# Attention and an ELU layer on one core: the order of the loads, the bank pair of unit 3, and the engines' written orders of two blocks

## The chip, the core and the metric

The kernel runs on one core of one Trainium2 chip. The metric is the device time of one execution in microseconds (us). The profile is of one execution; its engines are TensorE (PE, with its weight loads as PEld), VectorE (DVE), ScalarE (ACT), GpSimd (POOL) and SyncE (SP). All times below, unless said otherwise, count from the start of the profiled span.

## The reference: what is computed

A linear attention over 8 batches x 8 heads x 576 rows x 64 columns, and behind it a layer of 512 to 2048 to 512 with an ELU between, for all 4608 rows:

```python
q_s = softmax of q over the 64 columns
k_s = softmax of k over the 576 rows
kv  = einsum('bhsd,bhde', transposed k_s, v)      # 64 x 64 for each head
x   = (q_s @ kv) with the heads side by side       # 4608 x 512
h   = x @ w_in                                     # 512 -> 2048
g   = h where h > 0, else exp(min(h, 0)) - 1
out = g @ w_out                                    # 2048 -> 512
```

Inputs and output are float32. (The two softmax lines are in words; the maxima that the reference takes off first are not needed with inputs of this size.)

## The kernel before: how the work is laid out

**Units.** The attention is done in 16 units. A unit is four of the eight heads of one batch (`n // 2` is the batch, `n % 2` the half): q, k and v tiles of 128 x 1152, 576 KB each. For a unit, ScalarE takes the exponentials of q and k; VectorE sums q (`L421`) and takes the RECIPROCAL (`L423`); Pool or VectorE makes the quotient in 16 bits (`L433`, tile QS); Pool or ScalarE turns v to bf16 (`stage1`, `L277`, tile VB). Then the quotient is transposed: for units 0 to 3 on TensorE into PSUM (`tp`, `L457`) and copied out to qsT (`L277`), for the later ones by a DMA from SP (`turn`, `L470`, tile QT) and a widening copy (`widen`, `L277`). TensorE multiplies k by v (`kv_mm`, `L507`), VectorE divides by the sums of k and writes the 64 x 64 results into a block mask (`m`, `L516` and `L520`, tile MBLK), TensorE multiplies mask and transposes (`ao_mm`, `L538`; for units 0 and 1 `ao_parts`, `L550`), in two parts called outputs below, and ScalarE or VectorE copies these into XT (`xt`, `L277`), the input of the layer.

**Blocks.** The layer is done in nine blocks of 512 rows. A block has eight groups: a group is 8 matmuls on W1 into a pair of PSUM banks (`hg_mm`, `L620`), then the ELU (`hg`): the exponential on ScalarE (`L646`), and either a Relu on ScalarE and one operation on VectorE (`L648`, `L652`) or two on VectorE (`L657`, `L659`). The results are in GR. Blocks 0 and 1 multiply GR by W2 in the plain way (`out_mm`, `L673`): block 0 in four tiles of rows (ts) by four quarters of W2, 4 matmuls each; block 1 in pieces of two. From block 2 on, a scheme with sums and differences does it (`pair`, `L806`, `L757`, `L815`).

**Banks.** PSUM has 8 banks, b0 to b7, in four pairs. b6 and b7 (AB = 3 in `program`) are the side banks, which the attention takes from unit 2 on; b4 and b5 (C = 2) serve the groups and the rows' outputs and are lent to the attention here and there. Before, unit 3's transposes and its first output use b4 and b5; its product of k and v and its second output use b6 and b7.

**Order.** The program makes a list of operations, `S.ops`, each with what it reads and writes. The order on each engine is written out by hand in `ORDER`, as numbers of that list; `order()` times it with costs only to interleave the engines and to place spare matmuls at the start (`fill`, `spare_until`), and `emit()` puts in the waits. So an engine runs its line in the written order, and an instruction that waits holds up all that stand behind it on its engine. DMAs issued by Pool (`load`, `load_w1`, `load_w2`) stand in Pool's line among its copies and products and run one behind the other; later loads, the turns and the stores are issued by SP. `AFTER` adds four waits on Pool, which are the same operations before and after the change.

The numbers below are those of before. What matters of them:

- 14 to 17: W1 for groups 0 to 2, one for each 128 of its 512 rows; 18, 19, 20, 21: W1 for group 3, 4, 5, and 6 with 7. 69, 70, 74, 75: W2's four quarters. 68, 71, 72 and 73, 76, 77: q, k, v of units 2 and 3. 131, 144, 132 and 163, 164, 205: q, v, k of unit 4 and q, k, v of unit 5; 206: q of unit 6 (SP).
- Unit 2: 114 (exponential of q), 115 (of k), 117, 118 (sums, RECIPROCAL), 119, 120 (product, 640 and 512 columns), 116 (v), 125, 126 (transposes, copy), 127 to 130 (k times v, mask), 145, 146 and 151, 152 (outputs and their evictions).
- Unit 3: 137, 138 (exponentials), 140 to 143 (sums, RECIPROCAL, products), 139 (v), 153, 154 (transposes, copy), 159 to 162 (k times v, mask), 165 to 167 and 172 to 174 (outputs, evictions).
- Block 0: 78 to 89 groups 0 to 2 in parts of two matmuls; 147 to 150, 155 to 158, 168 to 171 and 175 to 178 the tiles on W2's quarters 1 to 4; 179, 182, 185, 188 the copies of the four tiles to SBUF (OSBX), stored by SP.
- Block 1: 191 to 194 groups 0 and 1 in halves; 253, 259, 266, 272, 279, 285 groups 2 to 7; 267 to 269 the ELU of group 4.
- Units 4 to 6: 201, 202, 203 and 225, 226, 227 sums, RECIPROCAL and product of units 4 and 5; 204 and 228 their turns; 210 and 230 their widening; 231 the first output of unit 5; 297 the exponential of unit 6's q.

The written order of TensorE from block 0's last W1 group to the start of block 1's fourth:

```
121 107 147 148 155 156 149 125 150 158 157 127 153 168 145 171 169 151
176 175 170 177 159 178 172 165 192 194 191 193 253 259 258 257 265 211 264 266
```

Of the kernel before, what the change touches and what calls it, by code (L numbers as in the profile page):

```python
# [49 lines left out]
    "act": (  # L50
# [12 lines left out]
    "dve": (  # L63
# [211 lines left out]
class Gen:  # L275
# [586 lines left out]
    def program(self):  # L862
# [41 lines left out]
        for t in "kv":  # L904
            self.load(3, t, -26)
# [78 lines left out]
        key = 0  # L984
# [105 lines left out]
```

## Time and profile before

| | us |
|---|---|
| median of 3 runs | 292.28 |
| lowest, highest | 292.17, 292.68 |
| span of the profiled execution (first to last instruction) | 290.4 |
| TensorE busy in it | 280.6 |
| VectorE, ScalarE, Pool busy | 225.5, 209.7, 167.8 |

The profiled execution's own time is the 290.4 of its span; the runs' times hold some more around it, 292.28 - 290.4 = 1.9 for the median. In the page, a group of instructions is named by the line of the kernel that emits it, the engine, the operation, and the tiles that it writes and reads (`PS<-XT,W`: PSUM from XT and a weight); L277 is a helper that copies, so the tile tells which copy it is. The bracket behind a row of the timeline gives the idle time of the engine before it and what ended it.

### The profile page before, as it was taken

Reading aid. Unit: us, or ns where it says so; the run is one execution under the profiler, and the core shown is the slowest. Engines: PE = TensorE matmul, PEld = TensorE weight load, DVE = VectorE, ACT = ScalarE, POOL = GpSimd, SP = SyncE. Lnnn points to the kernel's source line nnn. Section 1 sums busy time; section 2 is a strip of 40 time slices with the busy share of each in tenths; the row PEclk is TensorE's granted clock in tenths of the full one; section 3 lists DMA queues with packets and bytes.
Section 4 is the critical chain, followed back from the end, with each engine's and each line's share of the span. In section 5 each row is a group of like instructions: output and inputs, shape, how many; then the busy total and the mean of one; then the engine's idle time right before and its main releaser. Section 6 shows DMA issues by size and latency. Waiting matters only on the chain.

```text
span 290.4 us, 5465 instructions
## 1 busy us (share of the span) xinstructions
PE 280.6 (97%) x2176; PEld 243.7 (84%) x2176; DVE 225.5 (78%) x425; ACT 209.7 (72%) x237; POOL 167.8 (58%) x161
## 2 busy tenths in 40 slices
PE   2899999999999999999999999999999999999995
PEld 0488787778888899989999988989999999988995
DVE  3758834777699978989996987688977786794884
ACT  4857839989899899968995598975385656665510
POOL 1991335523869778676574886757314234277741
PEclk9999999999999999999999999999999999999999
DMA  7999999798896838739939295313102002300334
GB/s 259 399 363 390 389 389 339 163 260 323 238 349 163 241 91 228 202 78 305 178 96 222 56 292 129 76 40 71 46 18 56 0 2 67 78 2 1 92 73 128
DMA packets 36474, 50.04 MB, mean 172 GB/s; under 512 B 16352, under 2 KB 18144, under 8 KB 36448
## 3 DMA queue, kind: packets, MB, share of 16 engines
q1 hardware_dynamic: 29680, 33.96, 43.7%
q0 software_dynamic: 6528, 15.47, 17.8%
q8 instruction: 17, 0.28, 0.5%
q10 hardware_dynamic: 240, 0.26, 0.3%
q14 instruction: 9, 0.07, 0.1%
HBM read 36.70 MB, written 9.44 MB: 159 GB/s over the span
## 4 chain that ended last, share of the span: by engine, by line
PE 94%; DMA 2%; POOL 2%; SPq 0%; issue 0%; DVE 0%
PE PS L620 46%; PE PS L806 32%; PE PS L673 10%; PE PS L538 3%; DMA KR<-in_k_dram 2%; PE PS L507 2%; POOL W L377 1%; POOL VB L277 0%; PE PS L457 0%; POOL QS L433 0%; SPq L359 0%; PE PS L550 0%; DVE OSB L815 0%
## 5 line engine op out<-in xcount | busy, mean ns | idle before, releaser
L620 PE MATMUL PS<-XT,W 128*128 128x512 f32 x576 | 142.0, 393 | 0.1
L620 PEld LDWEIGHTS PS<-XT,W 128*128 128x128 f32 x576 | 105.0, 188 | 21.2 <-DVE GR L659 0.5
L652 DVE SCALAR_TENSOR_TENSOR GR<-PS,GE 128x512 fp32r<-128x512 f32 x112 | 76.8, 686 | 18.7 <-ACT GE L648 16.7
L646 ACT ACTIVATE GE<-PS 128x1024 f32<-128x1024 f32 x56 | 57.4, 1025 | 40.0 <-PE PS L620 34.2
L757 POOL TENSOR_TENSOR GR<-GR 128x256 fp32r<-128x256 f32 (+1 forms) x48 | 47.2, 996 | 31.5 <-DVE SB L757 16.6
L648 ACT ACTIVATE GE<-GE 128x1024 f32<-128x1024 f32 x56 | 59.4, 1061 | 1.4
L806 PE MATMUL PS<-W,GR 128*128 128x256 f32 x336 | 53.7, 283 | 0.0
L806 PE MATMUL PS<-TB,GR 128*128 128x256 f32 x336 | 51.3, 283 | 0.0
L806 PEld LDWEIGHTS PS<-W,GR 128*128 128x128 f32 x336 | 47.6, 191 | 1.7
L806 PEld LDWEIGHTS PS<-TB,GR 128*128 128x128 f32 x336 | 45.7, 191 | 0.7
L433 POOL TENSOR_TENSOR QS<-QR,RZQ 128x1152 f16<-128x1152 f32 (+1 forms) x16 | 30.4, 1898 | 21.4 <-DVE RZQ L423 19.7
L815 DVE TENSOR_TENSOR OSB<-OSB,PS 128x256 f32<-128x256 f32 x84 | 34.7, 416 | 10.3 <-PE PS L806 9.2
L673 PE MATMUL PS<-W,GR 128*128 128x512 f32 x128 | 32.7, 396 | 0.0
L757 POOL TENSOR_TENSOR GR<-SB,GR 128x256 fp32r<-128x256 f32 (+1 forms) x18 | 17.3, 971 | 24.6 <-PE PS L806 12.7
L673 PEld LDWEIGHTS PS<-W,GR 128*128 128x128 f32 x128 | 23.3, 188 | 5.0 <-DMA W<-in_moe_w_out_dram 0.5
L757 POOL TENSOR_TENSOR SB<-GR 128x256 fp32r<-128x256 f32 (+1 forms) x20 | 19.2, 965 | 13.7 <-DVE GR L652 6.4
L421 DVE TENSOR_REDUCE ZQ<-QR 128x18 f32<-128x1152 f32 (+2 forms) x18 | 21.7, 1207 | 6.1 <-ACT QR L419 4.8
L757 DVE TENSOR_TENSOR GR<-GR 128x256 fp32r<-128x256 f32 (+1 forms) x36 | 21.3, 603 | 0.6 <-PE PS L806 0.6
L277 POOL CAST VB<-VR 128x1152 bf16<-128x1152 f32 (+1 forms) x11 | 11.9, 1084 | 13.1 <-DMA VR<-in_v_dram 13.1
L646 ACT ACTIVATE ESB<-PS 128x1024 f32<-128x1024 f32 x16 | 16.1, 1024 | 4.5 <-PE PS L620 3.4
L399 ACT ACTIVATE KR<-KR 128x1152 bf16<-128x1152 f32 x16 | 18.4, 1155 | 0.8 <-DMA KR<-in_k_dram 0.8
L277 ACT ACTIVATE XT<-PS 128x512 fp32r<-128x512 f32 (+6 forms) x23 | 13.6, 595 | 6.3 <-PE PS L538 3.2
(58 smaller groups left out, 271.4 us busy)
## 6 DMA issues: line engine op xcount, KB each, us to landing
out_dram<-OSB SPq DMA_DIRECT2D x61, 128.0 KB, 2.4
QR<-in_q_dram SPq DMA_DIRECT2D x12, 576.0 KB, 4.9
KR<-in_k_dram SPq DMA_DIRECT2D x12, 576.0 KB, 6.3
VR<-in_v_dram SPq DMA_DIRECT2D x12, 576.0 KB, 5.1
W<-in_moe_w_out_dram POOLq DMA_DIRECT2D x4, 1024.0 KB, 16.7
QR<-in_q_dram POOLq DMA_DIRECT2D x4, 576.0 KB, 12.1
VR<-in_v_dram POOLq DMA_DIRECT2D x4, 576.0 KB, 13.0
KR<-in_k_dram POOLq DMA_DIRECT2D x4, 576.0 KB, 11.1
```

The source lines that it names most:

```text
L277: return e.activation(dst, src, AF.Copy) if e is self.nc.scalar else e.tensor_copy(dst, src)
L399: S.add("act", t_act(1152, False), lambda e: e.activation(ek[:, :, :, :].rearrange("p h c d -> p (h c d)"), flat(k), AF.Exp), key - 2, X=[ ...
L421: S.add("dve", t_dve(m), lambda e, qp=qp, zp=zp: e.tensor_reduce(zp, qp, AX.X, ALU.add), key - 3, R=[f"qR{i}{x}" for x in xs], W=[f"ZQ{i}{ ...
L433: lambda e, qp=q[:, :, a:b, :], rz=rz, dst=qs[:, :, a:b, :]: e.tensor_tensor(dst, qp, rz, ALU.mult),
L620: last = e.matmul(P[:, t * 512:(t + 1) * 512], self.W1[:, kc, tt * 128:(tt + 1) * 128], self.XT[:, kc, rc:rc + BLK], start=(kc == 0), stop ...
L646: S.add("act", t_act(1024, True), lambda e: e.activation(ge, P, AF.Exp), key, W=own, X=banks)
L648: S.add("act", t_act(1024, False), lambda e: e.activation(ge, ge, AF.Relu, bias=1.0, scale=-1.0), key, X=own)
L652: S.add("dve", t_dve(512 if j else 1024), lambda e, u=u: e.scalar_tensor_tensor(*(x[:, :, u, :] if j else x for x in (gt, P)), 0.0, ge[:, ...
L673: last = e.matmul(dst, self.tile(jb, jj, ts), self.W2[:, jj, c0:c1], start=(jj == 0), stop=(jj == 15))
L757: lambda e: e.tensor_tensor(dst, a, b, op), key, R=R, W=W, X=X, after=after)
L806: last = e.matmul(dst, a[i][:, y_, :], b[i][:, y_, :], start=start and i == 0 and y_ == 0, stop=stop and i == len(grps) - 1 and y_ == z - ...
L815: S.add("dve", t_dve(256), lambda e: e.tensor_tensor(dst, a, b, ALU.add), key, R=R, W=W, X=X, after=after)
```

## The change

Five things are changed.

1. *W1.* The loads for group 4 and for group 5 (19, 20) become one of 1024 KB.
2. *W2.* `load_w2` takes a range of 128-row pieces. The last quarter becomes two halves of it (75a, 75b), each of 512 KB; what waits for W2 now waits for pieces of two. In the list they stand behind unit 3's keys and values.
3. *Block 0's last quarter.* Each of its four tiles (175 to 178) becomes two of 2 matmuls, a and b, for the two halves.
4. *Banks.* Unit 3's transposes and its first output use b6 and b7, too.
5. *ORDER.* All five lines are written anew. After renumbering (one load fewer, one more, four tiles more) SP's is the same, and the others are the same from the middle of block 1 on.

The code outside of ORDER:

```diff
-    def load_w2(self, s, key, after=()):
+    def load_w2(self, jj0, jj1, key):
...
-        sl = slice(s * 4, (s + 1) * 4)
+        sl = slice(jj0, jj1)
...
-                   W=[f"W2_{s}"], dma=f"w2{s}", nbytes=1 << 20, after=after)
+                   W=[f"W2_{s}" for s in range(jj0 // 2, jj1 // 2)], dma=f"w2{jj0}", nbytes=jj1 - jj0 << 18)
...
-                [f"W2_{s}" for s in range(jj0 // 4, (jj1 + 3) // 4)], X=[f"b{bk}"])
+                [f"W2_{s}" for s in range(jj0 // 2, (jj1 + 1) // 2)], X=[f"b{bk}"])
...
-        return [f"W2_{s}" for s in range(z0 // 2, (z1 + 1) // 2)]
+        return [f"W2_{s}" for s in range(z0, z1)]
...
-        for g0, g1 in ((3, 4), (4, 5), (5, 6), (6, 8)):
+        for g0, g1 in ((3, 4), (4, 6), (6, 8)):
...
-        self.load_w2(2, -27)
-        self.load_w2(3, -25)
+        self.load_w2(8, 12, -27)
         for t in "kv":
             self.load(3, t, -26)
+        for jj in (12, 14):
+            self.load_w2(jj, jj + 2, -25)
...
-            ps, eng = (C if x == 0 else AB, "both") if n == 3 else (AB, "act")
+            ps, eng = AB, "both" if n == 3 else "act"
...
-                return n, lambda: self.tp(n, C if n == 3 else AB, due(n) - 4, ("act",))
+                return n, lambda: self.tp(n, AB, due(n) - 4, ("act",))
...
-                self.out_mm(0, ts, (ts + 2) % 4, 4 * jq, 4 * jq + 4, key)
+                for jj in range(4 * jq, 4 * jq + 4, 2 if jq == 3 else 4):
+                    self.out_mm(0, ts, (ts + 2) % 4, jj, jj + (2 if jq == 3 else 4), key)
```

The lines of ORDER after the change, in the numbers of before, as far as they differ:

```
TensorE  33 35 37 52 56 54 60 57 78 79 64 65 82 81 84 87 85 88 80 83 86 89 99 103 110 133
         121 107 147 148 155 156 150 125 149 158 127 157 145 169 151 171 168 153 170 175a
         176a 159 175b 176b 178a 165 178b 177a 172 192 194 177b 191 193 253 259 257 264
         258 265 211 266
ScalarE  3 29 25 41 22 45 24 38 34 40 53 55 59 66 90 93 94 96 100 101 104 111 112 114 108
         122 109 134 115 137 146 135 138 182 166 198 173 224 249 250 195 199 207 254 260
         261 297 267
VectorE  30 26 31 27 28 42 43 36 44 46 49 50 47 51 48 58 61 62 63 67 ... 113 117 118 123
         124 126 128 129 130 140 141 142 152 136 154 160 161 162 179 167 188 174 201 225
         202 185 251 252 196 197 255 256 212 262 213 263 226 214
Pool     1 32 14 23 16 15 17 39 18 19+20 21 68 69 70 71 72 73 74 77 76 120 119 116 75a 75b
         143 131 163 139 144 132 164 200 205 203 208 210 227
```

and before, the same stretches of the other engines:

```
ScalarE  3 29 25 41 22 36 23 45 53 34 38 39 58 66 90 93 94 96 100 101 104 111 112 114 108
         122 134 109 137 135 126 115 146 154 152 138 179 182 198 185 188 173 166 224 249
         250 195 207 199 254 260 261 210 267 297
VectorE  30 31 26 42 27 43 44 28 46 47 49 50 51 59 55 61 62 63 67 ... 113 117 123 118 124
         119 140 141 136 142 128 129 130 160 161 162 174 167 201 202 225 226 251 252 196
         197 255 256 262 263 212 213 214
Pool     1 32 14 15 24 16 17 18 48 40 19 20 21 69 68 70 73 72 71 74 75 76 77 120 131 116
         143 163 144 139 132 164 200 205 203 208 227
```

Operations that change engines: from ScalarE to VectorE the copies 36, 58 (unit 0), 126, 152, 154 and block 0's copies 179, 185, 188; from ScalarE to Pool the v copies 23 and 39 (640 columns) and unit 4's widening 210; from Pool to ScalarE the v copies 24 and 40 (512 columns); from Pool to VectorE unit 1's product 48 (512); from VectorE to Pool unit 2's product 119 (640); from VectorE to ScalarE the copies 55 and 59. Pool's order of issue of the loads changes as its line shows: unit 2's q ahead of W2's first quarter, unit 3's v and k ahead of W2's last quarter, and that quarter's halves behind unit 2's products and v copy.

More of the change, by code (lines that the diff above doesn't have):

```diff
@@ L27 @@
     "pe": (
[22 rows of a table removed]
-    "act": (
[12 rows of a table removed]
-    "dve": (
[37 rows of a table removed]
[23 rows of a table added]
+    "act": (
[11 rows of a table added]
+    "dve": (
[37 rows of a table added]
 }
-AFTER = ((208, 196), (227, 255), (234, 268), (300, 281))
+AFTER = ((212, 200), (231, 259), (238, 272), (304, 285))
 class Op:
@@ L885, in program @@
         self.side(0, -3, self.kv_mm(1, 0))
-        kv1 = S.ops[-1]
+        S.spare_until = S.ops[-1]
         self.m(1, 0, -12)
-        S.spare_until = S.ops[-4]
         self.ao_parts(1, 0, -2)
@@ L897, in program @@
         self.load(2, "q", -28)
-        self.load_w2(0, -29)
-        self.load_w2(1, -29)
+        self.load_w2(0, 4, -29)
+        self.load_w2(4, 8, -29)
         for n, t in ((2, "k"), (2, "v"), (3, "q")):
             self.load(n, t, -28)
-        self.load_w2(2, -27)
-        self.load_w2(3, -25)
+        self.load_w2(8, 12, -27)
         for t in "kv":
             self.load(3, t, -26)
+        for jj in (12, 14):
+            self.load_w2(jj, jj + 2, -25)
         def due(n):
```

138 rows, old and new, of the table ORDER are left out of this document.

## The prediction

> **What bounds the kernel now.** I read the page first (busy shares), then windows by stage, then what TensorE's weight loads wait for.
>
> ```profile
> span 290.4 us, 5465 instructions
> PE 280.6 (97%) x2176; PEld 243.7 (84%) x2176; DVE 225.5 (78%) x425; ACT 209.7 (72%) x237; POOL 167.8 (58%) x161
> ```
>
> ```profile
> 13.80:29.50 15.70, 15.70 (x105) 13.04 (x105) 11.26 (x15) 10.39 (x12) 9.43 (x13) 1.00 1.47 379
> 29.50:72.00 42.50, 42.41 (x337) 33.33 (x337) 27.74 (x44) 34.74 (x42) 17.55 (x16) 1.00 1.04 308
> 72.00:271.40 199.40, 199.40 (x1542) 178.50 (x1541) 166.31 (x319) 151.41 (x166) 124.25 (x110) 1.00 0.46 122
> ```
>
> The rows give window, length, busy time (instructions) of TensorE, its weight loads, VectorE, ScalarE and Pool, then TensorE's granted clock. TensorE bounds the kernel from 13.8 us on, at full clock. From 72 us it is busy to the last hundredth, and the diff moves nothing there. So the change can win only what TensorE loses before 72. Recorded times of matmuls overlap, so I count starts:
>
> ```profile
> 16.32 13.16 PE PS L620 x58
> ```
>
> ```profile
> 31.80 0.77 PEld L673 LDWEIGHTS PS<-W,GR 128*128 128x128 f32 x4 [0.46 <-DMA W<-in_moe_w_out_dram]
> 54.04 1.69 PEld L620 LDWEIGHTS PS<-XT,W 128*128 128x128 f32 x8 [0.46 <-DVE GR L652]
> 58.95 1.21 PEld L620 LDWEIGHTS PS<-XT,W 128*128 128x128 f32 x6 [0.47 <-DVE GR L659]
> ```
>
> ```profile
> 38.51 0.68 PE L457 MATMUL PS<-ID,QS 128*128 128x128 f16 x9
> 39.04 1.20 PE L673 MATMUL PS<-W,GR 128*128 128x512 f32 x4
> 40.08 0.46 PE L538 MATMUL PS<-qsT,MBLK 128*128 128x320 f32 x2
> 40.38 2.01 PE L673 MATMUL PS<-W,GR 128*128 128x512 f32 x8
> 48.28 7.88 PE L620 MATMUL PS<-XT,W 128*128 128x512 f32 x32
> ```
>
> The first row, of the chain, gives the pace: 13.16/58 = 0.227 from start to start. The weight loads show where that pace breaks (in the bracket: their idle time and who ended it): three times. What one break costs: eight matmuls take 2.01 = 7 x 0.227 + 0.42, so the 32 from 48.28 on, with the break at 54.04 among them, would take 31 x 0.227 + 0.42 = 7.46; they take 7.88. That is 0.4, and some of it belongs to a small gap elsewhere; I take 0.3 for a break, 0.2 of waiting and 0.1 of refilling. The refill shows alone at 39.04, where four matmuls behind 16-bit transposes take 1.20 instead of 3 x 0.227 + 0.42 = 1.10. So the three breaks hold 0.9 us (at most 1.3): 0.3% of the run is the ceiling. None is a wait for W2's last quarter or for unit 3's keys and values.
>
> **The change part by part.** *The loads.* They stand in one Pool queue and land one behind the other: issues (start, length), then size and us to landing.
>
> ```profile
> 13.56 2.28 POOL L377 DMA_DIRECT2D W<-in_moe_w_in_dram  x3
> 17.26 0.80 POOL L385 DMA_DIRECT2D W<-in_moe_w_out_dram  x1
> 20.16 1.58 POOL L385 DMA_DIRECT2D W<-in_moe_w_out_dram  x2
> ```
>
> ```profile
> W<-in_moe_w_in_dram POOLq DMA_DIRECT2D x1, 512.0 KB, 5.7
> W<-in_moe_w_in_dram POOLq DMA_DIRECT2D x1, 512.0 KB, 6.4
> W<-in_moe_w_out_dram POOLq DMA_DIRECT2D x1, 1024.0 KB, 14.5
> W<-in_moe_w_out_dram POOLq DMA_DIRECT2D x1, 1024.0 KB, 18.8
> W<-in_moe_w_out_dram POOLq DMA_DIRECT2D x1, 1024.0 KB, 20.7
> ```
>
> The two 512 KB pieces of W1 land at 13.56 + 5.7 = 19.3 and, issued 0.8 later, at 20.8: 1.5 apart, 3.0 for both. W2's third and fourth quarters land at 20.16 + 18.8 = 39.0 and, issued 0.8 later, at 41.7: 2.7 for 1024 KB in rows as long as the merged piece's. Merging saves 0.3 for all that lands behind it. Against it, Pool now copies 640 columns instead of 512 of units 0's and 1's values, ahead of issuing W1's later pieces, and the queue may run dry for 0 to 0.3. I take 0.15, so what lands behind comes 0.15 sooner (bounds 0 and 0.3): W2's second quarter at 31.6 instead of 17.26 + 14.5 = 31.76, its third at 38.8. Unit 3's keys and values move up by one quarter, 2.7; W2's last eighth lands at 44.5. I cost these moves at nothing: TensorE asks for that eighth at 44.8 (below), and had other work while ScalarE and Pool waited for unit 3.
>
> The Trainium skill (DMA: Bandwidth & Descriptors, section Bandwidth) has it that transfers be batched to 1 MiB or more, and the section on the anatomy of a DMA issued by GpSimd gives each a fixed 2.0 us. By that rule two halves would end some 2 us behind one whole; the rows here disagree, with 512 KB pieces landing 1.5 apart. It stays as the last rival.
>
> *The start (units 0 and 1).* Nine copies and products change engines. With the durations that they had I find block 0's matmuls 0.05 later (bounds 0.3 sooner, 0.4 later); the group of two matmuls (0.45) that no longer stands in front comes back behind. The break at 31.8 hides it: TensorE now comes there at 31.80 - 0.2 + 0.05 = 31.65, the quarter lands at 31.6. That break goes, and 0.15 + 0.1 = 0.25 is gained.
>
> *Block 0's last part.* Unit 3's transposes (153; 39.04 - 38.51 = 0.53) now stand behind the first use of W2's third quarter, and unit 2's first output (145; 40.38 - 40.08 = 0.30) ahead of it. One more change from 16-bit to f32 matmuls comes ahead too (0.1). TensorE so asks for that quarter at 39.04 - 0.53 + 0.30 + 0.1 - 0.25 = 38.66, and it lands at 38.8: **what was gained at 31.8 is given back here**, 0.15 to 0.2 of waiting; the refill takes the place of the one that stood at 39.04. At the start of block 1 (48.28) I get -0.25 + 0.1 + 0.2 = 0.05 lost (bounds 0.3 gained, 0.4 lost).
>
> *One pair of banks.* Unit 3's transposes, product and both outputs now take banks 6 and 7 in turn, each behind the eviction of the one before, and VectorE has six evictions of ScalarE's.
>
> ```profile
> 38.64 0.17 DVE L516 RECIPROCAL RZK<-PS 128x2 f32<-128x2 f32 x1 [0.55 <-PE PS L507]
> 38.84 0.61 DVE L520 TENSOR_TENSOR MBLK<-PS,RZK 64x128 fp32r<-64x128 f32 x2
> ```
>
> ```profile
> L277 ACT ACTIVATE qsT<-PS 128x1152 fp32r<-128x1152 f16 x2 | 2.3, 1135 | 1.4 <-PE PS L538 1.4
> L277 DVE CAST qsT<-PS 128x512 fp32r<-128x512 f16 x1 | 0.7, 680 | 0.0
> L421 DVE TENSOR_REDUCE ZQ<-QR 128x18 f32<-128x1152 f32 x5 | 6.7, 1340 | 1.2 <-ACT QR L395 1.2
> L433 DVE TENSOR_TENSOR QS<-QR,RZQ 128x640 f16<-128x640 f32 x4 | 3.3, 855 | 0.0
> ```
>
> VectorE's copy of 1152 columns out of PSUM is in no row: at least ScalarE's 1.14, at most 0.68 x 1152/512 = 1.53; I take 1.35, the smaller row's 0.68 with its fixed part kept once. Unit 2's wide product goes from VectorE (0.86) to Pool, where it is longer, but its q is one quarter earlier in the queue and its RECIPROCAL one place earlier on VectorE: nothing. Unit 2's product (127) comes one tile (0.9) and 0.25 sooner than here, so its mask, ready at 38.84 + 0.61 = 39.45 here, is ready at 38.3. Behind it on VectorE, with 0.04 between: unit 3's sums 1.34, RECIPROCAL 0.27, product 0.86, eviction of unit 2's second output 0.68 (done 41.6), block 0's last ELU 1.2 (as long as the row at 62.86 below), copy of unit 3's transposes 1.35: 44.25. TensorE comes to the transposes at 42.0, needing 41.6, and to unit 3's product (159) at 44.4, needing 44.25 and 0.06 for the hand-over. That costs nothing, but the cover is 0.1; past it each tenth is lost. Taken as 0 (bounds 0 and 0.6 lost).
>
> *Block 1.* A group of two matmuls of block 0 (0.45) now stands between the two groups of block 1 that met the break at 54.04: that one goes, 0.3. The one at 58.95 hangs on ELUs of the same chain and comes 0.3 sooner with it. Then:
>
> ```profile
> 54.93 0.57 SPq L359 DMA_DIRECT2D QR<-in_q_dram  x1
> 60.06 1.54 SPq L470 DMA_TRANSPOSE QT<-QS  x1
> ```
>
> ```profile
> QR<-in_q_dram SPq DMA_DIRECT2D x1, 576.0 KB, 5.0
> QT<-QS SPq DMA_TRANSPOSE x1, 7.5
> ```
>
> ```profile
> 58.83 1.15 ACT L277 ACTIVATE qsT<-QT 128x1152 fp32r<-128x1152 f16 x1
> 61.07 1.03 ACT L646 ACTIVATE ESB<-PS 128x1024 f32<-128x1024 f32 x1 [1.09 <-PE PS L620]
> 61.99 1.16 ACT L395 ACTIVATE QR<-QR 128x1152 f32<-128x1152 f32 x1
> ```
>
> ```profile
> 62.13 0.69 DVE L657 TENSOR_SCALAR ESB<-ESB 128x1024 f32<-128x1024 f32 x1 [0.19 <-ACT ESB L646]
> 62.86 1.22 DVE L659 TENSOR_TENSOR GR<-ESB,PS 128x1024 fp32r<-128x1024 f32 x1
> 64.41 1.98 PE L620 MATMUL PS<-XT,W 128*128 128x512 f32 x8
> ```
>
> Unit 6's exponential (297, at 61.99) moves ahead of that of block 1's group 4 (267, at 61.07), to where unit 4's widening stood (58.83), which goes to Pool. It waits for unit 6's q: 54.93 + 5.0 = 59.9, and 60.1 after the change, as unit 5's sums are put ahead of unit 4's RECIPROCAL and so of the turn ahead of that load. So 297 runs from 60.15 to 61.3, and 267, whose matmuls end at 60.8, starts at 61.2. Its ELU ends 1.03 + 0.69 + 1.22 and hand-overs later: 64.25. Group 6 (64.41) needs that ELU's banks: it starts at 64.3 at the soonest and refills for 0.1. **Whatever is won by then, some 0.25, ends here.**
>
> *Sum:* -0.25 (31.8) + 0.3 (switch and third quarter) - 0.3 (54 and 58.95) + 0.25 (exponential) = 0, and 0.1 for loads that may land later than I took: 290.5 for the span of 290.4. The median shown, 292.28, stands 1.85 above this span; so 292.4.
>
> **The rivals.**
>
> *No wall at 64* (15%). If q lands by 59.6, the exponential ends before group 4's matmuls do, and 0.25 to 0.6 stays: 292.1. Against it are the 5.0 of this load; for it, that it rides behind a turn, whose length varies.
>
> *Loads well ahead* (10%). If W2's second and third quarters land 0.5 or more sooner than I have them, the first break goes, no new one comes, and all 0.9 is won: 291.4. The steps of 2.7 and 1.5 in the rows speak against it.
>
> *The bank pair is the bound* (18%, slower). Place: VectorE's line from unit 2's mask to the copy of unit 3's transposes, 5.95 us. If its operations cost a tenth more, or the copy 1.53, it ends 0.2 to 0.6 later; past the cover of 0.1 all of it is lost, and block 1 with its q load is later by as much: 293.0. Six evictions more on VectorE speak for it.
>
> *A late turn* (10%, slower). Unit 5's RECIPROCAL goes behind block 1's ELU of group 3, to 60.5; its product on Pool, then 2.1, ends at 62.9, and the turn (60.06) goes out at 63.0, with a store and units 6's and 7's keys behind it on SP. Unit 5's first output, at 69.2, needs the turn landed by 67.9. With 7.5 as here it lands at 70.5 and 2.5 is lost: 294.9. Likelier is the median:
>
> ```profile
> QT<-QS SPq DMA_TRANSPOSE x12, 4.1
> ```
>
> *Each half pays for itself* (2%, slower). If W2's last eighth carried a latency of its own, it would land 2 later, at 46.5, TensorE wanting it at 44.8: 294.0. (That is the page's rule above.)
>
> **How the numbers follow.** The forecast has 45%: 292.4, by itself 291.9 to 292.8. What a measurement tells from no change is 0.2%, 0.58 us: 291.70 and 292.86. Faster: the loads' case and a fifth of the first rival, 13%. Slower: the last three, 30%. Within: the rest, 57%. The range, 291.4 to 293.5, leaves out the late turn, the last rival and the worst of the bank pair.
>
> **What would show it.** Right: the idle 0.46 at 31.8 gone, a wait for W2's third quarter near 38.8, none at 54, ScalarE waiting for unit 6's q to 60.1, the weight loads waiting for an ELU near 64.3. Wrong: no wait at 38.8 or 64.3 and a shorter span; VectorE's copies releasing TensorE between 42 and 45; or a wait for unit 5's outputs near 69.

## The result, and the profile after

The changed kernel takes 293.35 us (median of 5 runs, 293.11 to 293.57), the kernel before 292.17 beside it (5 runs, 291.98 to 292.68): the ratio is 1.004, with a 95% interval of 1.0027 to 1.0052. So it is slower by 0.4%. The time lies in the predicted range, but on the slower side, not in the likeliest case (292.4, no difference that can be told). The span of the profiled execution grew from 290.4 to 291.3, and TensorE's clock is full in both. (The medians lie 1.2 apart, the two profiled executions 0.9; the traces can explain the 0.9.)

First the head of the page, and the three windows of the prediction for the changed kernel:

```profile
span 291.3 us, 5465 instructions
PE 281.1 (96%) x2177; PEld 243.8 (84%) x2177; DVE 232.5 (80%) x431; ACT 205.4 (71%) x230; POOL 170.5 (59%) x162
```

```profile
13.80:29.50 15.70, 15.70 (x107) 12.94 (x105) 11.19 (x14) 11.99 (x13) 7.98 (x11) 1.00 1.35 386
29.50:72.00 42.50, 42.06 (x335) 32.95 (x334) 32.86 (x49) 28.58 (x33) 21.55 (x20) 1.00 0.97 300
72.00:271.40 199.40, 199.40 (x1541) 178.40 (x1540) 166.25 (x318) 151.67 (x166) 124.67 (x109) 1.00 0.46 124
```

From 72 us on nothing moved. All that changed lies ahead of it. In the middle window VectorE's busy time rose from 27.74 to 32.86, and TensorE's fell from 42.41 to 42.06. TensorE's weight loads show where its pace breaks now (idle time and who ended it in the bracket):

```profile
34.19 0.77 PEld L673 LDWEIGHTS PS<-W,GR 128*128 128x128 f32 x4 [0.64 <-DVE GR L659]
39.16 0.30 PEld L538 LDWEIGHTS PS<-qsT,MBLK 128*128 128x128 f32 x2 [0.23 <-DVE MBLK L520]
40.52 0.30 PEld L538 LDWEIGHTS PS<-qsT,MBLK 128*128 128x128 f32 x2 [0.30 <-ACT XT L277]
59.45 3.51 PEld L620 LDWEIGHTS PS<-XT,W 128*128 128x128 f32 x16 [0.29 <-DVE GR L659]
65.14 1.69 PEld L620 LDWEIGHTS PS<-XT,W 128*128 128x128 f32 x8 [0.46 <-DVE GR L659]
```

Of the three breaks of before, those at 31.8 and 54 are gone, as they should be. There is a new one at 34.19, for an ELU; the one at 58.95 stands at 59.45; and one at 65.14 is where the prediction put its wall (64.3). Where TensorE stands, by the start of the same operations in each trace (us; numbers of before, as everywhere below; x4, x6, x7 and x8 are experiments):

| operation | before | after | x4 | x6 | x7 | x8 |
|---|---|---|---|---|---|---|
| 147, first tile on W2 | 29.68 | 30.05 | 29.77 | 29.56 | 30.19 | 30.00 |
| 155, first on W2's second quarter | 31.80 | 31.99 | 31.70 | 31.49 | 32.12 | 31.94 |
| 192, block 1 starts | 48.28 | 48.65 | 47.94 | 48.20 | 48.16 | 47.96 |
| 259 | 54.05 | 54.64 | 53.72 | 54.20 | 54.54 | 54.06 |
| 266 | 58.95 | 59.45 | 58.62 | 58.82 | 58.96 | 58.60 |
| 279, group 6 | 64.41 | 65.14 | 64.11 | 64.68 | 64.49 | 64.09 |
| 283, behind it | 66.22 | 67.09 | 65.92 | 66.63 | 66.30 | 65.90 |

At 192 the changed kernel still has a group of two matmuls of block 0 (0.45) to do, so it is about 0.8 late there, not 0.37. It is 0.37 late already at 147; then the break at 34.19 adds to it. At 283 it is 0.87 late, and that is the 0.9 of the span.

Three places make up what the prediction lacked. First VectorE and Pool around 32 us (start, length):

```profile
31.48 1.40 DVE L657 TENSOR_SCALAR ESB<-ESB 128x1024 f32<-128x1024 f32 x1 [0.29 <-ACT ESB L646]
32.91 1.22 DVE L659 TENSOR_TENSOR GR<-ESB,PS 128x1024 fp32r<-128x1024 f32 x1
```

```profile
31.28 2.72 POOL L433 TENSOR_TENSOR QS<-QR,RZQ 128x512 f16<-128x512 f32 x2 [9.51 <-DVE RZQ L423]
```

The first half of the ELU (123) takes 1.40 instead of the 0.69 that it had before, while Pool works on unit 2's products (120, then 119, which the change gave it). The ELU's second half (124) ends at 34.13, and that is the break at 34.19. The product that 123 met is 120, which was Pool's before, too. Before, it ran behind 123:

```profile
31.51 0.69 DVE L657 TENSOR_SCALAR ESB<-ESB 128x1024 f32<-128x1024 f32 x1
```

```profile
32.46 1.04 POOL L433 TENSOR_TENSOR QS<-QR,RZQ 128x512 f16<-128x512 f32 x1 [9.24 <-DVE RZQ L423]
```

It waits for unit 2's RECIPROCAL (118). The change puts that ahead of 123 on VectorE, and so 120 runs at 31.28.

The same happens in the start: VectorE's product 28, 0.82 before, takes 1.64 here, beside Pool's 32.

```profile
7.11 1.64 DVE L433 TENSOR_TENSOR QS<-QR,RZQ 128x640 f16<-128x640 f32 x1
```

```profile
7.01 1.05 POOL L433 TENSOR_TENSOR QS<-QR,RZQ 128x512 f16<-128x512 f32 x1 [5.14 <-DVE RZQ L423]
```

Third, Pool's line around 42 us. Before, q and v of unit 4 were issued at 34.49 and 39.13:

```profile
34.49 0.74 POOL L359 DMA_DIRECT2D QR<-in_q_dram  x1 [0.98 <-DVE QS L433]
39.13 0.72 POOL L359 DMA_DIRECT2D VR<-in_v_dram  x1
```

After:

```profile
40.88 1.68 POOL L433 TENSOR_TENSOR QS<-QR,RZQ 128x512 f16<-128x512 f32 x1 [3.93 <-DVE RZQ L423]
42.52 1.49 POOL L359 DMA_DIRECT2D QR<-in_q_dram  x2
45.09 0.72 POOL L359 DMA_DIRECT2D VR<-in_v_dram  x1
```

These loads now stand behind unit 3's product on Pool (143), which waits 3.93 for VectorE's RECIPROCAL of unit 3 and then takes 1.68 instead of the 1.05 that it took before: it began inside VectorE's product 142 (40.83 to 41.66). The loads land 0.8 to 0.9 later (46.95 and 49.95 instead of 46.16 and 49.08). Unit 4's copy of v (200) and its product (203) follow as late on Pool, then the turn on SP (54.37 instead of 53.50), and behind it unit 6's q: issued at 56.17 instead of 54.93, landed at 61.00 instead of 59.91. Of these 1.24 at the issue, 0.87 is the turn's later start; the rest is that the turn's own issue took 1.76 instead of 1.38. So the wall of the prediction stands, 0.8 later than it had it:

```profile
61.02 1.17 ACT L395 ACTIVATE QR<-QR 128x1152 f32<-128x1152 f32 x1 [1.80 <-DMA QR<-in_q_dram]
62.10 1.01 ACT L646 ACTIVATE ESB<-PS 128x1024 f32<-128x1024 f32 x1
```

```profile
63.14 0.69 DVE L657 TENSOR_SCALAR ESB<-ESB 128x1024 f32<-128x1024 f32 x1 [0.91 <-ACT ESB L646]
63.87 1.22 DVE L659 TENSOR_TENSOR GR<-ESB,PS 128x1024 fp32r<-128x1024 f32 x1
```

Read from the top: ScalarE waits 1.80 for q, the exponential 297 runs, group 4's exponential 267 waits behind it though its matmuls were done at 61.4, its ELU ends at 65.09, and TensorE gets group 6's banks at 65.14.

### The profile page after: what moved, and what is told of

Read it like the earlier page. It is cut to its first block, busy times and chain, and to the rows that moved or that the text cites. A ratio compares the mean times of both kernels' runs of the same rounds, so it can differ in the third digit from the quotient of the medians.

```text
span 291.3 us, 5465 instructions
## 1 busy us (share of the span) xinstructions
PE 281.1 (96%) x2177; PEld 243.8 (84%) x2177; DVE 232.5 (80%) x431; ACT 205.4 (71%) x230; POOL 170.5 (59%) x162
## 4 chain that ended last, share of the span: by engine, by line
PE 90%; DVE 5%; ACT 2%; DMA 1%; issue 0%
PE PS L620 44%; PE PS L806 32%; PE PS L673 8%; PE PS L538 3%; PE PS L507 2%; DMA QR<-in_q_dram 1%; DVE GR L659 1%; DVE QS L433 1%; ACT ESB L646 1%; DVE ESB L657 1%; PE PS L457 1%; DVE ZQ L421 1%; DVE GR L652 0%; ACT ESB L648 0%; PE PS L550 0%
## 5 line engine op out<-in xcount | busy, mean ns | idle before, releaser
L433 POOL TENSOR_TENSOR QS<-QR,RZQ 128x1152 f16<-128x1152 f32 (+2 forms) x16 | 31.5, 1972 | 25.7 <-DVE RZQ L423 25.6
L395 ACT ACTIVATE QR<-QR 128x1152 f32<-128x1152 f32 x14 | 16.2, 1160 | 3.9 <-DMA QR<-in_q_dram 3.9
L277 ACT ACTIVATE OSB<-PS 128x256 f32<-128x256 f32 (+1 forms) x21 | 7.9, 387 | 13.5 <-PE PS L806 13.5
```

Source lines behind the costliest of these rows:

```text
L395: S.add("act", t_act(1152, False), lambda e: e.activation(flat(q), flat(q), AF.Exp), key - 3, X=[f"qR{i}0", f"qR{i}1"])
L433: lambda e, qp=q[:, :, a:b, :], rz=rz, dst=qs[:, :, a:b, :]: e.tensor_tensor(dst, qp, rz, ALU.mult),
```

## The experiments

Theories at the outset: (1) the exponential 297 waiting for q sets the end; (2) Pool's products beside VectorE's operations do, in block 0's last part; (3) unit 4's late loads do, since they make q late. From the first four runs came a fourth, the one that is called several walls: the causes stand one behind the other, and to take one away uncovers the next. The edits are given in ORDER, in the numbers of before. In the experiments' profiles the kernel's lines are numbered 10 or 11 higher (L667 and L669 are the ELU's two halves, in x11 L668 for the first). A span is that of one profiled execution. Those of the changed kernel, x1, x5, x6 and x11 were the fastest of their runs, that of x10 the slowest; and those of x1, x2 and x3 reached block 0's first tile on W2 (147) 0.20, 0.11 and 0.31 later than the changed kernel's, where the load of unit 0's k had landed later, too (8.08, 7.80 and 8.04 instead of 7.70). So a difference of 0.1 or 0.2 between two spans says little by itself.

| | median, us | ratio to before, 95% interval | span |
|---|---|---|---|
| changed kernel | 293.35 | 1.004 (1.0027 to 1.0052) | 291.3 |
| x1 exponential back | 293.40 | 1.0052 (1.0039 to 1.0066) | 291.3 |
| x2 unit 2's products back | 292.97 | 1.0028 (1.0018 to 1.0038) | 291.2 |
| x3 unit 4's loads sooner | 293.20 | 1.0037 (1.0026 to 1.0049) | 291.4 |
| x4 before, W1 merged | 292.06 | 0.9996 (0.9988 to 1.0005) | 290.2 |
| x5 x1 and unit 5's RECIPROCAL | 293.12 | 1.0036 (1.0023 to 1.0048) | 290.9 |
| x6 start back | 292.87 | 1.0025 (1.0016 to 1.0034) | 290.8 |
| x7 x1, x2, x3 and the RECIPROCAL | 292.35 | 1.0010 (0.9997 to 1.0022) | 290.5 |
| x8 x7 and the start | 291.81 | 0.9988 (0.9980 to 0.9997) | 290.0 |
| x9 x8, two pairs of banks | 292.63 | 1.0018 (1.0009 to 1.0027) | 290.8 |
| x10 changed, two pairs of banks | 294.11 | 1.0075 (1.0062 to 1.0087) | 292.9 |
| x11 before, product 119 on Pool | 292.39 | 1.0011 (1.0002 to 1.0020) | 290.1 |
| x12 changed, 31 ahead of 26 | 293.35 | 1.0050 (1.0030 to 1.0070) | 291.5 |

### x1: the exponential back

```diff
 ScalarE
-260 261 297 267
+260 261 267 297
```

> The changed kernel with one move: unit 6's exponential (297) stands behind that of block 1's group 4 (267) again on ScalarE. Theory 1 (the exponential that waits for q until 61.0 sets the end): 267 starts when its matmuls end, about 61.5 instead of 62.1; the weight loads' wait of 0.46 at 65.1 goes; TensorE is late by what it was late at 59.45, 0.5, and the span falls from 291.3 to about 290.9 (ratio to before near 1.002). Theory 2 (the lateness comes from block 0's last part and the exponential only fills a pause): the span stays at 291.2 to 291.3, with a wait of the same length somewhere behind.

Measured: 267 ran 0.4 sooner, at 61.70, and the span stayed at 291.3. The 0.4 was lost at the next instruction, on VectorE:

```profile
62.77 1.19 DVE L667 TENSOR_SCALAR ESB<-ESB 128x1024 f32<-128x1024 f32 x1 [0.38 <-ACT ESB L656]
63.99 1.22 DVE L669 TENSOR_TENSOR GR<-ESB,PS 128x1024 fp32r<-128x1024 f32 x1
```

```profile
61.29 2.12 POOL L443 TENSOR_TENSOR QS<-QR,RZQ 128x1152 f16<-128x1152 f32 x1 [1.81 <-DVE RZQ L433]
```

268 takes 1.19 instead of 0.69. Pool's product of unit 5 (227) runs beside it to 63.41, since the change put unit 5's RECIPROCAL (226) behind block 1's ELUs. Theory 1 falls as the only cause: behind the wall stands another of the same height.

### x2: unit 2's products back

```diff
 VectorE
-117 118 123 124 126
+117 123 118 124 119 126
 Pool
-76 120 119 116
+76 120 116
```

> The changed kernel with unit 2's products as before: the RECIPROCAL (118) behind block 0's ELU of group 6 (123), the wide product (119) on VectorE behind 124. Theory 2 (Pool's product beside VectorE's TENSOR_SCALAR doubled that one, 1.40 instead of 0.69, and broke TensorE's pace at 34.19): 123 takes 0.69 again, 124 ends at 33.4 instead of 34.13, the wait of 0.64 at 34.19 goes, and the start of block 1 (48.65) comes 0.3 to 0.5 sooner. Theory 1: the span nevertheless stays within 0.2 of 291.3, since unit 6's exponential still ends near 62. A pure theory 2 has the span at 290.8 to 291.0.

Measured: 123 is back at 0.70, the break at 34.19 is gone, and TensorE is 0.43 sooner from 34 to 58 us. Then it waits 0.90, for the ELU of the group before 266:

```profile
56.82 1.37 DVE L667 TENSOR_SCALAR ESB<-ESB 128x1024 f32<-128x1024 f32 x1 [1.09 <-ACT ESB L656]
58.22 1.22 DVE L669 TENSOR_TENSOR GR<-ESB,PS 128x1024 fp32r<-128x1024 f32 x1
```

```profile
56.49 1.15 POOL L287 CAST VB<-VR 128x1152 bf16<-128x1152 f32 x1 [2.61 <-DMA VR<-in_v_dram]
```

255 takes 1.37 beside Pool's copy of unit 5's v (208), which waited for that v to 56.4: one of the loads that came late. 266 starts at 59.49, no sooner than in the changed kernel. Theory 2 is right at its place and does not reach the end by itself. (The median fell by more than the span; the two intervals overlap.)

### x3: unit 4's loads sooner

```diff
 Pool
-75a 75b 143 131 163 139 144 132
+75a 75b 131 144 143 163 139 132
 VectorE
-201 225 202 185
+201 202 225 185
```

> The changed kernel with unit 4's q and v loads (131, 144) ahead of unit 3's Pool product (143) in Pool's line, and unit 4's RECIPROCAL (202) ahead of unit 5's sums (225) on VectorE. Theory 3 (the chain of unit 4's v, its copy, its product, its turn and then unit 6's q is what made the exponential late): v of unit 4 lands at 47 to 48 instead of 49.95, unit 4's product starts near 51.0 instead of 52.2, unit 6's q lands near 59.9 instead of 61.0, the exponential ends by 61.1, group 6 of block 1 starts 0.5 to 0.6 sooner than 65.14, span near 290.8. If the q is late for another reason (its own transfer), it lands above 60.6 and the span stays at 291.2.

Measured: v of unit 4 landed at 47.23 instead of 49.95, unit 6's q at 59.87 instead of 61.00, and 297 was done at 61.06, before 267 could start. So the chain of theory 3, from those loads to the late exponential, is as stated. The span is 291.4 all the same: 268 began at 62.72 inside Pool's 227 (61.39 to 63.51) and took 1.34.

### x4: the kernel before with W1 merged

```diff
-        for g0, g1 in ((3, 4), (4, 5), (5, 6), (6, 8)):
+        for g0, g1 in ((3, 4), (4, 6), (6, 8)):
```

> The kernel before with one part of the change alone: W1's loads for groups 4 and 5 merged. My step: all that lands behind comes 0.3 sooner (W2's second quarter at 31.45 instead of 31.76), the wait of 0.46 at 31.8 goes or shrinks to under 0.2, W2's third quarter lands at 38.7 and TensorE is 0.2 to 0.3 ahead at 39. Carried to the end: span 290.1 to 290.2 (0.2 to 0.3 under 290.4). If the breaks behind it (54, 58.95) grow instead, the span stays at 290.4.

Measured: the break at 31.8 is gone, TensorE is 0.3 sooner at 279 and 283, and the span is 0.2 shorter. The times, 0.06 apart, do not tell it from no change. Nor is it shown that the merge did it: in the profiled execution of x11 (below), with W1 in two loads as before, the break at 31.8 is gone as well. There W2's second quarter landed at 31.49, against 31.76 in the kernel before and 31.26 here. So this load lands 0.27 apart from one execution to the next without any merge, and the merge's own part in the 0.3 stays open.

### x5 and x7: two walls, four walls

x5 is x1, with unit 5's RECIPROCAL (226) ahead of 251 on VectorE, so that Pool's 227 runs sooner. x7 is x1, x2, x3 and that edit together.

```diff
 VectorE
-185 251 ... 263 226 214
+185 226 251 ... 263 214
```

> The changed kernel with two places back: unit 6's exponential (297) behind the one of group 6 (267) on ScalarE, and the reciprocal of unit 5 (226) behind unit 4's division work on VectorE (ahead of 251), so that GpSimd can run unit 5's product (227) before 268. Theory of several walls one behind another: 267 at 61.7, 268 back to 0.69 us (62.8 to 63.5) and 269 done at 64.7, so group 6 (279) starts when TensorE itself gets there, 65.05 instead of 65.14 (65.27 in x1), and its refill of 0.14 goes: span 291.0 (between 290.9 and 291.1), since the half microsecond that TensorE has lost before 59.5 stays. Theory that GpSimd beside VectorE is all of the loss: 290.4 to 290.6. Theory that neither counts (the pair of banks): 291.3, 268 still over 1 us or TensorE late for another reason.

> The changed kernel with four places back together: 297 behind 267; 118 and 119 of unit 2 on VectorE behind 123 and 124; the loads of unit 4's q and v (131, 144) ahead of unit 3's product (143) on GpSimd, with 202 ahead of 225; 226 ahead of 251. Theory of several walls: no break at 34.2, 123 in 0.69, 255 and 268 in 0.69, 266 at 59.0, 279 at 64.3 to 64.5, span 290.2 to 290.5 (0.8 to 1.1 below the changed kernel), although unit 3 still has one pair of banks. Theory that the pair of banks (or the start) carries the loss: 291.0 or more, with 192 at 48.5 or later.

Measured: in x5, 227 ran 59.16 to 61.28, 268 took 0.69 and 279 started at 64.78; span 290.9. In x7 the four places all went as expected: 123, 255 and 268 take 0.69, 0.69 and 0.70, 266 starts at 58.96, 279 at 64.49, the span is 290.5.

```profile
31.62 0.69 DVE L667 TENSOR_SCALAR ESB<-ESB 128x1024 f32<-128x1024 f32 x1 [0.59 <-ACT ESB L656]
```

```profile
56.96 0.69 DVE L667 TENSOR_SCALAR ESB<-ESB 128x1024 f32<-128x1024 f32 x1 [1.10 <-ACT ESB L656]
62.20 0.70 DVE L667 TENSOR_SCALAR ESB<-ESB 128x1024 f32<-128x1024 f32 x1 [0.38 <-ACT ESB L656]
```

Alone, x1 left the span as it was, x2 took off 0.1 and x3 added 0.1; together with the RECIPROCAL they take off 0.8, and 1.0 of the median (293.35 to 292.35). That is what the theory of several walls says, and the traces show each wall at its place. The medians by themselves would not prove it: x2, x3 and x5 take off 0.38, 0.15 and 0.23, which is 0.76 in all, and the intervals are too wide to tell that from 1.0.

### x6 and x8: the start

x6 gives the changed kernel the start of before: the order and the engines of the operations up to block 0's first product, with W1 still merged. x8 is x7 with that start.

```diff
 VectorE
-30 26 31 27 28 42 43 36 44 46 49 50 47 51 48 58 61 62 63 67
+30 31 26 42 27 43 44 28 46 47 49 50 51 59 55 61 62 63 67
 Pool
-1 32 14 23 16 15 17 39 18 19+20 21
+1 32 14 15 24 16 17 18 48 40 19+20 21
```

(and TensorE's and ScalarE's lines up to 89 and 66 likewise).

> The changed kernel with the order and the engines of the first 16 us (up to block 0's first product of the attention output) as before the change; the merged load of W1 stays. Theory of several walls: TensorE is 0.35 sooner from 19 to 31 (147 at 29.7 instead of 30.05), and the lead is taken back by the later walls, above all by group 6 waiting for unit 6's exponential at 62.1: 279 at 65.0 to 65.15, span 291.1 to 291.3. Theory that the start is what the change lost: 0.35 sooner to the end, 290.9 or less.

> x7 with the start of x6 as well: what is left of the change is the merged W1, unit 3's keys and values ahead of W2's last quarter in two halves, and unit 3 in one pair of banks. Theory of several walls: another 0.2 to 0.35 sooner than x7, span 289.9 to 290.2, under the kernel before. Theory that the pair of banks costs on its own: no lead over x7 from 39 on, and a span of 290.4 or more.

Measured: in x6, 147 starts at 29.56, 0.49 sooner than in the changed kernel, although the first loads landed alike (unit 0's second tile at 7.69 and 7.70). The expectation that later walls would take it back was wrong: 279 is 0.46 sooner, span 290.8. The walls are links of the same chain and moved with it: Pool's and VectorE's lines began sooner, the turn's issue took 1.39 instead of 1.76, and unit 6's q landed at 60.11. What makes that issue 1.37 to 1.39 in ten of the fourteen traces and 1.76 to 2.13 in the other four stays open. (The medians are 0.48 apart, but the two intervals overlap a little.)

x8 has a span of 290.0 and is faster than the kernel before, by 0.12% (0.03% to 0.20%): x6's 0.5 and x7's 0.8 add up. Not all of that can be read at one place: x8's first loads landed 0.5 later than x6's, so 147 is at 30.00; and of its lead over x7, 0.2 is there at 192, and the rest comes at 253, where x7 waits for one of block 0's copies.

### x9 and x10: the pair of banks

Both give unit 3's transposes and its first output back the banks b4 and b5, x9 in x8 and x10 in the changed kernel; the orders stay.

```diff
-            ps, eng = AB, "both" if n == 3 else "act"
+            ps, eng = (C if x == 0 else AB, "both") if n == 3 else (AB, "act")
...
-                return n, lambda: self.tp(n, AB, due(n) - 4, ("act",))
+                return n, lambda: self.tp(n, C if n == 3 else AB, due(n) - 4, ("act",))
```

> x8_all_back with unit 3's transposes and its first output product in the other pair of banks, as before the change (orders kept). Theory that one pair of banks costs little (the rows of x8 show TensorE all but full between 36 and 48): 145 and 151 a tenth of a microsecond sooner each, 192 at 47.8 to 47.95, span 289.8 to 290.1, no difference from x8 that the times can tell. Theory that the pair of banks holds a real part of the loss: 192 at 47.5 or sooner and a span of 289.6 or less.

> The changed kernel with only unit 3's pair of banks as before. Theory of several walls: 291.1 to 291.3, no break goes. Theory that the pair of banks sets it: 290.4 to 290.7.

Both were missed, on the other side: the second pair makes each of the two slower, by 0.8 in both medians (x9 against x8, x10 against the changed kernel). In x9 TensorE's transposes (153) wait for VectorE:

```profile
42.83 0.51 PEld L467 LDWEIGHTS PS<-ID,QS 128*128 128x128 f16 x9 [1.12 <-DVE GR L662]
```

```profile
41.56 1.21 DVE L662 SCALAR_TENSOR_TENSOR GR<-PS,ESB 128x1024 fp32r<-128x1024 f32 x1
```

That is 136, the ELU that empties b4 and b5 of a group whose matmuls were done at 27.8. The new order puts it behind unit 3's sums and product; before, it ran at 36.05. So under the new order the second pair is emptied too late; with the side banks alone the later ELU does no harm. (x10's profiled execution also started 0.6 late, at 147; its span is not all from the banks.)

### x11: Pool beside VectorE in the kernel before

```diff
 VectorE
-117 123 118 124 119 140
+117 118 123 124 140
 Pool
-77 120 131
+77 120 119 131
```

> The kernel before with one thing of the change alone: unit 2's product 119 on GpSimd (behind 120) and 118 ahead of 123 on VectorE. Theory that GpSimd's products stretch VectorE's operations with both operands in SBUF: 123 takes 1.3 to 1.45 us instead of 0.69 although the kernel before has no other part of the change, 124 ends at 34.0 to 34.2 instead of 33.45, its reader on TensorE (149 and 150, 33.78 and 35.19 before) comes late by 0.2 to 0.5; the span grows by 0.1 to 0.5, 290.5 to 290.9. Theory that 123 was long in the changed kernel for another reason: 123 in 0.69 and 290.4.

Missed, and it told most. 123 was not stretched, though all of its second part ran beside Pool:

```profile
31.57 0.63 DVE L668 TENSOR_SCALAR ESB<-ESB 128x1024 f32<-128x1024 f32 x1
```

```profile
31.74 2.58 POOL L444 TENSOR_TENSOR QS<-QR,RZQ 128x512 f16<-128x512 f32 x2 [8.51 <-DVE RZQ L434]
```

This time VectorE began first, at 31.57, and Pool's 120 behind it, at 31.74. It was Pool that took longer: 120 ended at 33.10, after 1.36 instead of 1.05, 0.90 past the end of 123. So the two do not share the way to memory half and half: who begins second waits until the first is done.

This profiled execution is the fastest of the eleven. The median is 0.36 above that of the kernel before, with an interval of the ratio (1.0002 to 1.0020) that lies just above 1. So the edit costs something over its runs; whether 123 meets 120 in the slower ones, as expected, no trace shows.

### x12: one collision in the start

```diff
 VectorE
-30 26 31 27 28
+30 31 26 27 28
```

> The changed kernel with one instruction of VectorE moved: the short one (31) that GpSimd's first multiplication (32) waits for goes ahead of 26, as before the change, so that 32 runs 0.65 sooner. In the changed kernel 32 ran 7.01 to 8.06 and VectorE's multiplication 28, which began at 7.11, ended 0.68 after it, at 8.74; TensorE's transposes (33) waited for that. Theory that an operation of VectorE that begins inside one of GpSimd's waits until that one has ended: 32 at 6.36 to 7.42, 28 ends at 8.1 (7.42 and 0.68), 33 at 8.2 instead of 8.80, and the start's loss mostly goes: 147 at 29.55 to 29.75 instead of 30.05, which then lasts to the end as it did in the run with the whole start back: span 290.8 to 291.0. Theory that the start was late by its order on other engines: 28 and 33 sooner as well, but 147 at 29.95 to 30.1 and 291.2 to 291.4.

Measured: 32 ran 6.41 to 7.46, and 28 ended at 8.14, 0.68 behind it, as expected. TensorE's transposes started at 8.20 instead of 8.80, and it was 0.4 sooner from 14 to 20 us. But 147 is at 29.90, 0.15 sooner, and the span is 291.5. VectorE, now ahead, ran its product 48 at another moment, and Pool ran into it:

```profile
12.12 0.69 DVE L443 TENSOR_TENSOR QS<-QR,RZQ 128x512 f16<-128x512 f32 x1
```

```profile
12.27 1.12 POOL L287 CAST VB<-VR 128x640 bf16<-128x640 f32 x1 [0.51 <-DMA VR<-in_v_dram]
13.33 2.23 POOL L387 DMA_DIRECT2D W<-in_moe_w_in_dram  x3
```

Pool's copy 39 took 1.12 instead of 0.72, so W1's loads behind it in Pool's line were issued 0.41 later. The merged one landed at 22.0 instead of 20.7, and TensorE waited for it at 103 (22.17). The later issue is 0.4 of these 1.3; the rest is spread (in x5, issued as in the changed kernel, it landed at 21.74). So the collision accounts for the late start up to 20 us; that it accounts for all of x6's gain is not shown.

## Why the prediction was right and wrong, step by step

- *The pace and the three breaks.* Right. At most 0.9 could be won; the breaks at 31.8 and 54 went. In x4 the first one's going is worth 0.2 to 0.3; that the merged load made it go is not shown (x11).
- *The loads.* Near enough in the profiled execution: W2's second quarter landed at 31.33 (31.6 said), the third at 38.58 (38.8), the last half at 44.12 (44.5). One execution does not show a gain, though: with these loads in the same order, x1, x2, x3 and x5 have the second quarter between 31.35 and 32.13. The halves are these rows (size, us to landing; the first half, then the median of both):

```profile
W<-in_moe_w_out_dram POOLq DMA_DIRECT2D x1, 512.0 KB, 7.4
W<-in_moe_w_out_dram POOLq DMA_DIRECT2D x2, 512.0 KB, 7.6
```

  They are issued 0.74 apart at 35.48 and land at 42.85 and 44.12, 1.27 apart. The last rival, a latency for each half, is out. The Trainium skill's rule (DMA: Bandwidth & Descriptors, section Bandwidth: batch to 1 MiB or more) does not show in a queue that is kept full.
- *The start, "with the durations that they had … 0.05 later (bounds 0.3 sooner, 0.4 later)".* This step failed: the start lost 0.37 at 147, 0.49 with equal loads (x6). The durations did not stay what they had been: 28 met Pool's 32. Undoing that meeting alone brought back 0.15 at 147 (x12); the rest of the start's loss is not traced to a place.
- *The wait for W2's third quarter.* It didn't come: TensorE got to that quarter at 39.57, not at 38.66, late by the start and by the break at 34.19, and the quarter was there.
- *Unit 2's wide product to Pool, and "its RECIPROCAL one place earlier on VectorE: nothing".* **This step failed.** The product was priced by Pool's own line, where it indeed hid. What failed is the other half, the RECIPROCAL put at nothing: it starts Pool's 120 before VectorE's 123. That is read from the trace, where 123 ended 0.55 behind the end of 120 (32.33), with 119 still to run; it cost 0.7 for 123, and from there 0.43 on TensorE (x2, which undoes both halves). The trace of before had a small place of this kind, hidden in the mean of 0.86 that was taken for VectorE's products: 142 took 0.96, beside Pool's 143, where others took 0.82.
- *The pair of banks.* The copy of 1152 columns took 1.36 (1.35 taken), VectorE's line ended at 44.80 (44.25), and TensorE came at 45.27. So it cost nothing, as taken, and the rival that made it the bound is out; but here TensorE was itself late. x9 and x10 do not price the pair against the kernel before: they show that the new orders, which put the ELU 136 late, lose 0.8 with the second pair.
- *Block 1.* The break at 54 went. The one at 58.95 was to come 0.3 sooner and came 0.5 later, on an ELU's first half (255) stretched to 0.89 by Pool's copy 208.
- *The exponential.* **Right in its mechanism, wrong in one term.** 297 waits for q, 267 waits for 297, 279 for 267's ELU, and what TensorE has gained by then ends there. But q came at 61.0, not at 60.1, and so 279 at 65.14, not at 64.3. The 0.2 that was added to q's landing counted the place of unit 5's sums on VectorE; it left out Pool's line, where unit 4's q and v had moved behind unit 3's product and so behind a RECIPROCAL that the change makes late (x3). Another 0.4 is the turn's longer issue, whose cause is open.
- *The late turn.* It went out at 63.28 (63.0 said) and landed 3.5 later, at 66.81, 1.1 ahead of the 67.9 that was needed: the median's side, as taken.
- *The sum.* 0.1 was forecast and 0.9 came. x6 gives 0.5 of it to the start. x7 gives 0.8 to four places together; none of them could be told in the time by itself. Against these 1.3 stand 0.4 of span (0.24 of the median) by which x8, with both undone, is shorter than the kernel before; which of the parts left in x8 gives them was not tested. The slower side had 30%, all of it for other mechanisms. That the time lies in the range is luck: the range reached so far up for the pair of banks, which cost nothing.

## What to carry to other kernels

When a change of order moves an operation of Pool or VectorE in time, look at what the other of the two does in that very stretch: the price was on the other engine. The products and copies that VectorE met (32, 120, 208, 227) had all been Pool's before; only their time had moved, with a RECIPROCAL or a load that they wait for. When a product moves ahead in an engine's line, follow every load that the same engine issues behind it. And when undoing one part changes nothing, undo it together with the next suspect before calling it innocent: here three edits moved the span by 0.1 at most alone and, with a fourth, took off 0.8 together.

## What the hardware showed that was not expected

VectorE's first half of an ELU (one operand of f32 in SBUF, 1024 columns) and Pool's tensor operations exclude each other. In all the traces of this case there are 19 in which the former began inside one of Pool's, more than 0.14 ahead of that one's end. It then ended 0.545 to 0.562 us behind that end, every time, and took 0.71 to 1.47 by how early it had begun; by itself it takes 0.69 (the median of 84). That is one waiting for the other, not two at half speed. VectorE's product of two SBUF tensors does the same (28 ended 0.68 behind Pool's end in the changed kernel and in x12). The other way round, Pool's operations end late when they begin inside one of these (143 in the changed kernel, 120 in x11, 39 in x12). The ELU's second half (L659), which has one operand in PSUM, takes its 1.22 beside Pool as well as without. So do VectorE's sums of q over 1152 columns, with one operand in SBUF: 66 of them began inside an operation of Pool's, and they took 1.33 to 1.35, as by themselves.

The Trainium skill (GPSIMD Engine Reference, section Specifications) says that the interfaces to SBUF are shared with VectorE, with contention for instructions that have two SBUF inputs or run in a two-port mode. The traces agree for the products of two SBUF tensors, and for the sums and the ELU's second half, which are neither and are not touched. That the ELU's first half runs in a two-port mode no trace says; its 0.69 for 1024 columns, against 1.34 for the sums' 1152, would fit it. That the wait is whole is what the traces here show.
